# A transformer block's forward and backward pass on one core: token-major q and k by TensorE in place of DMA transposes, and b2 added by VectorE in place of one-row matmuls

## The chip, the core and the metric

The kernel runs on one core of a Trainium2 chip. The metric is the device time of one execution in microseconds (us). The kernel before took 688.7 us (median of three runs, 688.36 to 696.13). One of these executions was recorded by the hardware profiler; its trace is what the readings below rest on.

The engines are called as the profile calls them: PE is TensorE (its weight loads are listed apart as PEld), DVE is VectorE, ACT is ScalarE, POOL is GpSimd, and SP is SyncE, which does nothing here but issue DMAs. SPq, POOLq and ACTq are the streams in which an engine issues DMAs.

## The reference

One pre-norm transformer block over 2048 tokens of 512 features, and the gradients of its output with respect to the input and all weights:

```python
h  = x + attention(layernorm(x)) @ wo          # 32 heads of 16 features
h2 = h + gelu(layernorm(h) @ w1 + b1) @ w2 + b2    # 1792 hidden features
# attention of token s: softmax over the 8 tokens s, s-2, ..., s-14 (those before 0 are masked)
#   logits = q[s] . k[s - 2w] * 16**-0.5 ;  o[s] = sum_w attn[w] * v[s - 2w]
out, vjp = jax.vjp(block, x, wqkv, wo, w1, b1, w2, b2)
return out, *vjp(grad_out)
```

Inputs and outputs are bf16.

## The kernel before

The tokens are worked on in four chunks of 512 (`NC = 4`, `CH = 512`), each of four tiles of 128 (`TPC`). Two layouts are used: feature-major (features on the 128 partitions, tokens along the free dimension, four groups `g` of 128 features) and token-major (tokens on the partitions).

**Phase 1** (0 to about 190 us) is the attention forward pass. `p1_ln` loads x, normalizes it on DVE, and turns it feature-major on PE (`to_fm`: 16 transposes into two PSUM tiles of the pool `psT`, each copied out by ACT). `p1_qk` and `p1_v` project q, k and v feature-major; ACT copies each 128x512 result from PSUM. `dots` multiplies q with eight shifted views of k on DVE (four operations of 128x4096) and sums over the features of a head on PE. `p1_sm1` and `p1_sm2` are the softmax. `p1_o` needs v token-major: v's rows are written to DRAM (`v_d`), and POOL gathers ten shifted rows per partition from there into the tile `R` (`gather_rows`, two gathers per chunk, two tiles). DVE multiplies R with the softmax coefficients (`band`, line 275), PE sums, ACT copies `ost`, POOL stores it, and `unperm` turns it feature-major. `p1_d` multiplies with wo, adds x, and computes the second layer norm; `p1_d2` turns that feature-major for phase 2. `p1_round` sets the program order: `dots(c+1)`, `p1_d(c-1)`, `p1_qk(c+2)`, `p1_o(c)` in two halves with `p1_v(c+1)` between, so that three chunks are in work at a time.

**Phase 2** (about 190 to 395 us) is the feed-forward part, forward and backward. `p2_h` makes the hidden units and gelu; `p2_rest` multiplies with w2, adds b2 and h (line 640 adds b2 as a matmul with one contracted row, line 641 adds h through the identity matrix), stores the output, and runs the backward pass through w2 and w1.

**Phase 3** (from about 395 us) is the attention backward pass. It gathers rows from the token-major q, k and output gradient (`q_d`, `k_d`, `go_d`) as phase 1 does from `v_d`, and fills PE with the weight gradients.

What the change touches:

- *Order of the features.* The band multiplication wants token-major rows in the order (feature within a head, head). The kernel before gets it by reordering the weights: the columns of wqkv are loaded into `wraw` and `wrav` and copied into `wqkv` in the new order by ACT (k and q, four copies) and POOL (v, two copies), and wo's rows are reordered by a DRAM-to-DRAM transfer into `woP_d`, from which phase 3 loads its transpose. As all groups `g` then hold the same heads in the same places, one summing matrix `S32` serves them all.
- *Token-major q and k* (`to_tm_store`, called through `p1_tm` right after `p1_qk`): per chunk and tensor, four DMA transposes from SBUF to SBUF issued by SP, and then SP's stores to DRAM. v does not go this way: `p1_v` transposes it on PE (line 395), ACT copies the result (`vtm`, line 398), SP stores it (line 400). The output gradient goes through `to_tm_pe` in the same manner.
- *The second layer norm's last step* (`layernorm` with `aj`): the multiplication with rstd and the addition of the mean's term, four operations of 128x512 per chunk, run on ACT (line 181); in the first layer norm they run on DVE (line 183).

Each engine executes its instructions in one fixed order. In phases 1 and 2 a scheduler at build time chooses that order from the dependencies and the program order; in phase 3 it is written out by hand. SP issues its DMAs in such an order too, and an instruction that waits holds up all behind it on its engine.

Of the kernel before, what the change touches and what calls it, by code (L numbers as in the profile page):

```python
# [36 lines left out]
def kernel(  # L37
# [70 lines left out]
    make_identity(nc, ident[:])  # L108
    S32 = const.tile([P, 32], BF16, name="S32")
    Sum4 = const.tile([P, P], BF16, name="Sum4")  # L110
    nSum4 = const.tile([P, P], BF16, name="nSum4")
    Sm = const.tile([P, 4, P], BF16, name="Sm")
    mk = const.tile([16, 2, 4, 32], BF16, name="mk")
    ones_row = const.tile([1, P], BF16, name="ones_row")
# [4 lines left out]
    V.memset(ones_row[:], 1.0)  # L119
# [5 lines left out]
    b2row = const.tile([1, D], BF16, name="b2row")  # L125
# [8 lines left out]
    woP_d = dram.tile([D, D], BF16, name="woP_d")  # L134
# [32 lines left out]
    def layernorm(wp, src, rstd_all, c, dst, aj=()):  # L167
        mv = wp.tile([P, TPC, 2], F32, name="mv", tag="mv", bufs=2)
        for j in range(TPC):
            st = wp.tile([P, 6], F32, name="st6", tag="st6", bufs=2)  # L170
            V.bn_stats(out=st[:], in_=src[:, j, :])
            V.bn_aggr(out=mv[:, j, :], in_=st[:])
        rs = rstd_all[:, c * TPC:(c + 1) * TPC]
        ve = wp.tile([P, TPC], F32, name="ve", tag="ve", bufs=2)
        V.tensor_scalar(out=ve[:], in0=mv[:, :, 1], scalar1=EPS, scalar2=None, op0=ALU.add)
        G.tensor_tensor(out=rs, in0=ve[:], in1=mhalf[:], op=ALU.pow)
        nm = wp.tile([P, TPC], F32, name="nm", tag="nm", bufs=2)
        V.scalar_tensor_tensor(out=nm[:], in0=mv[:, :, 0], scalar=-1.0, in1=rs, op0=ALU.mult, op1=ALU.mult)
        for j in range(TPC):
            if j in aj:  # L180
                A.activation(out=dst[:, j, :], in_=src[:, j, :], func=ACT.Identity, scale=rs[:, j:j + 1], bias=nm[:, j:j + 1])
            else:
                V.tensor_scalar(out=dst[:, j, :], in0=src[:, j, :], scalar1=rs[:, j:j + 1], scalar2=nm[:, j:j + 1],
                                op0=ALU.mult, op1=ALU.add)
# [24 lines left out]
    def to_tm_pe(fm, dst, c, stage):  # L209
        for j2 in range(TPC // 2):  # L210
            pt = TT("ptm")
            for jj in range(2):
                for g in range(4):
                    T.transpose(pt[:, jj * 512 + g * P:jj * 512 + (g + 1) * P],
                                fm[:, g, (2 * j2 + jj) * P:(2 * j2 + jj + 1) * P], ident[:])
            st = stage()
            A.copy(out=st[:], in_=pt[:].rearrange("p (a n) -> p a n", a=2))
            r = j2 * 2 * P
            SY.dma_start(out=dst[c][r:r + 2 * P, :].rearrange("(a p) d -> p a d", p=P), in_=st[:])
            if j2 == 0 and c > 0:  # L220
                SY.dma_start(out=dst[c - 1][CH:CH + RPAD, :], in_=st[0:RPAD, 0, :])

    def to_tm_store(wp, fm, off, dst, c, back, nb=2, stage=None):
        st = stage() if stage else wp.tile([P, TPC, D], BF16, name="tmst", tag="tmst", bufs=nb)
        for g in range(4):
            SY.dma_start_transpose(out=st[:, :, g * P:(g + 1) * P], in_=fm[:, g, off:off + CH])
        r = RPAD if back else 0
        SY.dma_start(out=dst[c][r:r + CH, :].rearrange("(a p) d -> p a d", p=P), in_=st[:])
        if back and c + 1 < NC:
            SY.dma_start(out=dst[c + 1][0:RPAD, :], in_=st[P - RPAD:P, TPC - 1, :])  # L230
        if not back and c > 0:
            SY.dma_start(out=dst[c - 1][CH:CH + RPAD, :], in_=st[0:RPAD, 0, :])
# [9 lines left out]
    def dots(wp, ql, kw_, L, mask):  # L242
        for g in range(4):
            pr = wp.tile([P, W, 512], BF16, name="pr", tag="prod", bufs=2 + (wp is not late))
            V.tensor_tensor(out=pr[:], in0=ql[:, g, :].unsqueeze(1).to_broadcast([P, W, 512]),  # L245
                            in1=_sub(kw_[:, g, PAD:PAD + 512], [[-DIL, W], [1, 512]]), op=ALU.mult)
            for hf in range(2):
                for w4 in range(4):
                    T.matmul(L[hf][32 * w4:32 * w4 + 32, :], lhsT=S32[:], rhs=pr[:, 2 * w4 + hf, :],
                             start=(g == 0), stop=(g == 3), skip_group_check=True)  # L250
        if mask:
            for hf in range(2):
                T.matmul(L[hf][:, 0:16], lhsT=mk[:, hf].rearrange("p a b -> p (a b)"), rhs=ident[0:16, 0:16],
                         start=False, stop=True, skip_group_check=True)
# [80 lines left out]
    def p1_ln(c):  # L335
# [3 lines left out]
        if c == 0:  # L339
            wraw = wff.tile([P, 2, DC, D], BF16, name="wraw", tag="w10", bufs=1)  # L340
            wrav = wff.tile([P, DC, D], BF16, name="wrav", tag="w18", bufs=1)
            raws = [wraw[:, 1], wraw[:, 0], wrav[:]]
            for i in (1, 0, 2):
                SY.dma_start(out=raws[i], in_=A_wqkv[:, i * D:(i + 1) * D].rearrange("(a p) j -> p a j", p=P))

            def by_dh(i, put, lo, hi):
                put(out=wqkv[:, :, i * D + lo * H:i * D + hi * H].rearrange("p a (d h) -> p a d h", h=H),
                    in_=raws[i].rearrange("p a (h d) -> p a d h", d=DH)[:, :, lo:hi, :])
            by_dh(1, A.copy, 0, 8)
            by_dh(1, A.copy, 8, 16)  # L350
            by_dh(0, A.copy, 0, 8)
            by_dh(0, A.copy, 8, 16)
            by_dh(2, G.tensor_copy, 0, 8)
            by_dh(2, G.tensor_copy, 8, 16)
        ln1 = early.tile([P, TPC, D], BF16, name="ln1", tag="ln1", bufs=2)
        layernorm(early, xt, rstd1, c, ln1, ())
# [13 lines left out]
    def p1_tm(c):  # L370
        to_tm_store(early, st_[c]["kt"], PAD, k_d, c, True)
        to_tm_store(early, st_[c]["qt"], 0, q_d, c, False)

    def p1_qk(c):
        qt = early.tile([P, 4, CH], BF16, name="qt", tag="qt", bufs=2)
        kt = early.tile([P, 4, PAD + CH], BF16, name="kt", tag="kt", bufs=2)
        if c == 0:
            V.memset(kt[:, :, 0:PAD], 0.0)
            G.dma_start(out=vf_d[:, :, 0:PAD], in_=kt[:, :, 0:PAD])
# [6 lines left out]
        p1_tm(c)  # L386

    def p1_v(c):
        vt = early.tile([P, 4, PAD + CH], BF16, name="vt", tag="vt", bufs=1)
        p1_proj(c, 2, vt, PAD)  # L390
        for j2 in range(TPC // 2):
            pt = TT("ptm")
            for jj in range(2):
                for g in range(4):
                    T.transpose(pt[:, jj * 512 + g * P:jj * 512 + (g + 1) * P],
                                vt[:, g, PAD + (2 * j2 + jj) * P:PAD + (2 * j2 + jj + 1) * P], ident[:])
            st = early.tile([P, 2, D], BF16, name="vtm", tag="vtm", bufs=2)
            A.copy(out=st[:], in_=pt[:].rearrange("p (a n) -> p a n", a=2))
            r = j2 * 2 * P + RPAD
            SY.dma_start(out=v_d[c][r:r + 2 * P, :].rearrange("(a p) d -> p a d", p=P), in_=st[:])  # L400
            if j2 == 1 and c + 1 < NC:
                SY.dma_start(out=v_d[c + 1][0:RPAD, :], in_=st[P - RPAD:P, 1, :])
        G.dma_start(out=vf_d[:, :, PAD + c * CH:PAD + (c + 1) * CH], in_=vt[:, :, PAD:PAD + CH])

# [61 lines left out]
    def p1_d(c):  # L466
# [11 lines left out]
        layernorm(late, ht, rstd2, c, ln2, (0,1,2,3))  # L478
# [6 lines left out]
    p1_ln(0)  # L485
    for j in range(4):
# [4 lines left out]
    for j in range(4):  # L491
        V.tensor_copy(out=Sm[32 * j:32 * j + 32, j, :], in_=Sum4[32 * j:32 * j + 32, :])
    G.memset(mk[:], 0.0)
# [15 lines left out]
    for a_, b_, t_ in w1:  # L509
        G.dma_start(out=t_[:], in_=B_w1[:, a_ * P:b_ * P].rearrange("(a p) f -> p a f", p=P))  # L510
    def p1_round(c):
        if c + 2 < NC:
            p1_ln(c + 2)
        if c == 0:
            for (d_t, r) in ((v_d[0], 0), (k_d[0], 0), (q_d[NC - 1], CH), (go_d[NC - 1], CH)):
                SY.dma_start(out=d_t[r:r + RPAD, :], in_=zrow[:])
            G.dma_start(out=woP_d[:].rearrange("(d h) n -> d h n", h=H), in_=A_wo.rearrange("(h d) n -> d h n", d=DH))
            SY.dma_start(out=b1b[:], in_=B_b1.rearrange("(f p) -> f p", p=P))
            SY.dma_start(out=b2row[:], in_=B_b2.rearrange("(a n) -> a n", a=1))
# [18 lines left out]
        p1_o(c, 1)  # L538
        if c == 1:
# [21 lines left out]
    def load_wT(name, src):  # L561
# [6 lines left out]
               h2s=([P, D], 2), gyr=([P, D], 2), junk=([P, D], 1), u=([P, D], 2),   # L568
# [57 lines left out]
    def p2_rest(c):  # L626
# [8 lines left out]
        load_rows(ln2, ln2_d, c)  # L635
        for j in range(TPC):
# [3 lines left out]
            T.matmul(ps[:], lhsT=ones_row[:], rhs=b2row[:], start=False, stop=False)  # L640
# [45 lines left out]
    def ga_sum(L, pr, g):  # L686
        for hf in range(2):
            for w4 in range(4):
                T.matmul(L[32 * w4:32 * w4 + 32, hf, :], lhsT=S32[:], rhs=pr(2 * w4 + hf),
# [10 lines left out]
    def p3_pre():  # L700
# [7 lines left out]
        to_tm_pe(got, go_d, 0, lambda: ft("tst", "tmst0")[:, 0:8, :].rearrange("p (a b) f -> p a (b f)", a=2))  # L708
        yield
        L = [X("ps_ga0") for _ in range(2)]  # L710
        for g in range(4):
            pr = ft("xa", "pr0")
            ga_prod(pr[:].rearrange("p a b n -> p (a b) n"), got, vw, g)
            for hf in range(2):
                for w4 in range(4):
                    w = 2 * w4 + hf
                    T.matmul(L[hf][32 * w4:32 * w4 + 32, :], lhsT=S32[:], rhs=pr[:, w // 4, w % 4, :],
# [33 lines left out]
    for a_, b_, t_ in w2T:  # L751
        SY.dma_start_transpose(out=t_[:], in_=B_w2[a_ * P:b_ * P, :])
    goT0 = [ft("goT")]
# [29 lines left out]
    for c in range(NC):  # L783
        if c == 2:
            load_wT("woT", woP_d[:])
# [280 lines left out]
    def p3_go(c, at=(1, 2, 3, 4)):  # L1066
# [12 lines left out]
        def t():  # L1079
            to_tm_pe(got, go_d, c, lambda: pt3("tmst"))  # L1080
# [181 lines left out]
```

## Time and profile before

| what | us |
| --- | --- |
| median of three runs | 688.7 |
| the profiled execution | 688.36 |
| its span, first to last instruction | 686.5 |
| PE busy | 605.8 (88%) |
| DVE busy | 511.7 (75%) |
| ACT busy | 372.0 (54%) |
| POOL busy | 148.7 (22%) |
| mean granted PE clock | 0.968 of full |

The 1.9 us between the execution's time and its span lie before the first and after the last instruction. In rows of the trace the columns are: line of the kernel, engine, operation, the tile written and the tiles read (`out<-in`), shape; then busy time and the mean of one in ns, or, in a timeline, start and duration in us. What stands after `<-` in brackets or at a row's end is how long the engine had been idle before that row and what it had waited for. A timeline joins neighbouring instructions of one line into one row (`x2`). A wait for several things is put down to the one that came last.

### The profile page before, as it was taken

The numbers are of one execution on the slowest core, as the hardware profiler recorded it, in microseconds if no ns is written. First come the engines' busy times: TensorE is split into PE (matmuls) and PEld (weight loads), VectorE is DVE, ScalarE is ACT, GpSimd is POOL, SyncE is SP. The second block draws the span as 40 slices with busy tenths as digits, with TensorE's granted clock in tenths as the row PEclk, the third lists the DMA queues.
The fourth block names the chain that finished last, engine by engine and source line by source line (L and its number), as shares of the span: only waits on it lengthen the run. The fifth ranks groups of instructions, "written<-read, shape, count | busy, mean of one in ns | idle before, by whom it ended". The sixth has DMA issues, their size and how long they took to land. (4 is left out here: it accounts for less than half of the span.)

```text
span 686.5 us, 9972 instructions
## 1 busy us (share of the span) xinstructions
PE 605.8 (88%) x3761; PEld 281.1 (41%) x3820; DVE 511.7 (75%) x734; ACT 372.0 (54%) x574; POOL 148.7 (22%) x186
## 2 busy tenths in 40 slices
PE   2888838687699999999999988999999999988997
PEld 1333313233234444444444432434446567533443
DVE  7988838876878886986956878886978798396400
ACT  6576636669976366366333162594377337464311
POOL 6232122243201110110110115130223125030100
PEclk9999969789989999999999999999999999999999
DMA  7989999753699994995995899977599689979141
GB/s 234 232 237 286 232 227 199 270 175 112 150 254 255 249 256 100 236 252 151 238 275 151 230 353 331 362 249 279 181 394 324 240 285 354 322 271 314 70 153 47
DMA packets 165230, 163.58 MB, mean 238 GB/s; under 512 B 111757, under 2 KB 149694, under 8 KB 158526
## 3 DMA queue, kind: packets, MB, share of 16 engines
q1 hardware_dynamic: 137358, 73.78, 43.6%
q0 software_dynamic: 15520, 78.15, 33.6%
q10 hardware_dynamic: 12304, 11.01, 5.0%
q8 instruction: 30, 0.49, 0.3%
q14 instruction: 18, 0.15, 0.1%
HBM read 88.15 MB, written 48.55 MB: 199 GB/s over the span
## 5 line engine op out<-in xcount | busy, mean ns | idle before, releaser
L1045 DVE TENSOR_TENSOR prb<-R,cf 128x2048 bf16<-128x2048 bf16 x96 | 110.9, 1218 | 7.0 <-DMA R<-k_d,rowi 3.0
L189 ACT ACTIVATE gyr<-ps_gl,rstd 128x512 bf16<-128x512 f32 x32 | 21.9, 686 | 84.3 <-PE ps_gl L1108 32.0
L607 PE MATMUL ps_h<-ln2T,w 128*128 128x512 bf16 x219 | 57.1, 394 | 1.3 <-ACT xa L609 0.6
L929 PE MATMUL ps_gw<-gout_r,gwm 128*128 128x512 bf16 x216 | 52.8, 387 | 3.3 <-DMA gwm<-gT_d 2.8
L639 PE MATMUL ps_f<-w,gt 128*128 128x512 bf16 x220 | 53.0, 387 | 2.7 <-ACT ln2T L165 2.0
L652 PE MATMUL ps_gg<-goT,w2T 128*128 128x512 bf16 x219 | 53.9, 379 | 0.6 <-issue 0.2
L937 PE MATMUL ps_gw<-gwm,ln_r 128*128 128x256 bf16 x448 | 53.0, 273 | 1.0 <-ACT gwst L856 1.0
L663 PE MATMUL ps_gl<-w1T,dt 128*128 128x512 bf16 x218 | 50.9, 379 | 0.8 <-ACT gyr L189 0.4
L366 PE MATMUL ps_qkv<-ln1T,wqkv 128*128 128x512 bf16 x185 | 48.3, 399 | 3.7 <-ACT ln1T L165 2.6
L275 DVE TENSOR_TENSOR prb<-R,cf 128x2048 bf16<-128x2048 bf16 x32 | 37.6, 1212 | 18.7 <-DMA R<-v_d,rowi 18.7
L683 DVE TENSOR_TENSOR pr<-got,vw 128x4096 bf16<-128x4096 bf16 x16 | 36.3, 2289 | 16.2 <-ACT got L680 11.4
L654 DVE CUSTOM_DVE_ANT_0 dt<-ps_gg,dt 128x512 bf16<-128x512 f32 x56 | 37.7, 685 | 13.4 <-PE ps_gg L652 8.4
L937 PEld LDWEIGHTS <-ln_r 128*128 128x128 bf16 x448 | 42.6, 98 | 12.4 <-issue 6.5
L608 ACT ACTIVATE xb<-ps_h,b1c 128x512 bf16<-128x512 f32 x56 | 39.0, 698 | 11.6 <-PE ps_h L607 8.8
L957 PE MATMUL ps_gwq<-gqh,ln_r 128*128 128x512 bf16 x188 | 42.2, 379 | 0.8 <-ACT gwst L856 0.6
L609 ACT ACTIVATE xa<-ps_h,b1c 128x512 bf16<-128x512 f32 x56 | 38.9, 701 | 5.0 <-DVE dt L620 5.0
L592 POOL DMA_DIRECT2D gT_d<-tst x16 | 12.1, 755 | 123.7 <-DMA tst<-gt 123.3
L1055 ACT ACTIVATE gks<-ps_band 128x512 bf16<-128x512 f32 x32 | 19.0, 597 | 36.0 <-PE ps_band L1053 31.5
L245 DVE TENSOR_TENSOR pr<-qt,kt 128x4096 bf16<-128x4096 bf16 x16 | 35.9, 2283 | 0.7 <-PE ps_band L280 0.4
L293 ACT COPY gqkvT<-ptu 128x1024 bf16<-128x1024 bf16 x24 | 24.3, 1011 | 18.6 <-PE ptu L292 18.6
L607 PEld LDWEIGHTS <-w 128*128 128x128 bf16 x224 | 22.2, 101 | 29.4 <-issue 6.8
L614 ACT ACTIVATE xa<-xa 128x2048 bf16<-128x2048 bf16 (+1 forms) x16 | 27.2, 1697 | 13.0 <-DVE xa L613 12.9
(181 smaller groups left out, 1117.8 us busy)
## 6 DMA issues: line engine op xcount, KB each, us to landing
gwm<-ghT_d SPq DMA_DIRECT2D x7, 1024.0 KB
gT_d<-tst POOLq DMA_DIRECT2D x12, 512.0 KB, 4.7
ghT_d<-tst POOLq DMA_DIRECT2D x12, 512.0 KB, 4.8
gwm<-gT_d SPq DMA_DIRECT2D x6, 1024.0 KB
out_dram<-gwst ACTq DMA_DIRECT2D x22, 256.0 KB
ln_d<-ln POOLq DMA_DIRECT2D x8, 512.0 KB, 7.6
vw<-vf_d SPq DMA_DIRECT2D x4, 528.0 KB
xt<-in_A_x_dram SPq DMA_DIRECT2D x4, 512.0 KB
```

The source lines that it names most:

```text
L366: T.matmul(ps[:], lhsT=wqkv[:, dc, sel * D + g * P:sel * D + (g + 1) * P], rhs=st_[c]["ln1T"][:, dc, :], start=(dc == 0), stop=(dc == DC - 1))
L607: T.matmul(ps[:], lhsT=wcol(w1, dc, f), rhs=ln2T[c][:, dc, :], start=(dc == 0), stop=(dc == DC - 1))
L608: A.activation(out=xb[:, f - f0, :], in_=ps[:], func=ACT.Identity, bias=b1c[:, f:f + 1])
L609: A.activation(out=x2[:, f - f0, :], in_=ps[:], func=ACT.Square, bias=b1c[:, f:f + 1])
L639: T.matmul(ps[:], lhsT=gts[f // 4][:, f % 4, j * P:(j + 1) * P], rhs=wrow(w2, f), start=(f == 0), stop=False)
L652: T.matmul(ps[:], lhsT=wcol(w2T, dc, f), rhs=goT[:, dc, :], start=(dc == 0), stop=(dc == DC - 1))
L654: V.tensor_tensor_reduce(out=dsl, in0=ps[:], in1=dsl, scale=1.0, scalar=0.0, op0=ALU.mult, op1=ALU.add, accum_out=gb1p[:, f, c:c + 1])
L663: T.matmul(ps[:], lhsT=dts[f // 4][:, f % 4, j * P:(j + 1) * P], rhs=wrow(w1T, f), start=(f == 0), stop=(f == FT - 1))
L929: yield from mm_pair("ps_gw2", lambda ps, o, u, i, t, k: T.matmul(ps[:], lhsT=g_[:, o, i * HN + t, :], rhs=gout_r[i][:, t, :], **k), MM, w ...
L937: yield from mm_pair("ps_gw1", lambda ps, o, u, i, t, k: T.matmul(ps[:, 256 * u:256 * u + 256].rearrange("p (a f) -> p a f", a=2), lhsT=ln ...
L957: yield from mm_pair("ps_gwq", lambda ps, o, u, i, t, k: T.matmul(ps[:], lhsT=ln1_r[i][:, t, (2 * d2 + o) * P:(2 * d2 + o + 1) * P], rhs=h ...
L1045: V.tensor_tensor(out=pr[:, 4 * hf:4 * hf + 4].rearrange("p j (d h) -> p j d h", h=H), in0=R[:, o:o + 4, :].rearrange("p j (d h) -> p j d ...
```

## The change

The features keep their natural order (head, feature). wqkv is loaded straight into place and wo is used as it is. The reordering moves into the transposes that make rows token-major: their second operand is a permutation matrix `Pmat` in place of the identity, and they write PSUM in runs of eight elements. One function, `to_tm_store`, now does this for q, k, v and the output gradient, on PE with copies on ACT and stores issued by SP. In the sums over a head's features, `S32` becomes one matrix per group (`Emat`). `p1_tm` moves from the end of `p1_qk` to the end of `p1_round`. The second layer norm's last step goes to DVE. b2 is loaded once, repeated over all partitions, and added to h by one DVE operation per chunk.

```diff
+    Pmat = const.tile([P, P], BF16, name="Pmat")
+    ind8 = const.tile([P, 8], BF16, name="ind8")
+    Emat = const.tile([P, 4, 32], BF16, name="Emat")
...
-            if j in aj:
-                A.activation(out=dst[:, j, :], in_=src[:, j, :], func=ACT.Identity, scale=rs[:, j:j + 1], bias=nm[:, j:j + 1])
-            else:
-                V.tensor_scalar(out=dst[:, j, :], in0=src[:, j, :], scalar1=rs[:, j:j + 1], scalar2=nm[:, j:j + 1],
-                                op0=ALU.mult, op1=ALU.add)
+            V.tensor_scalar(out=dst[:, j, :], in0=src[:, j, :], scalar1=rs[:, j:j + 1], scalar2=nm[:, j:j + 1],
+                            op0=ALU.mult, op1=ALU.add)
...
-    def to_tm_store(wp, fm, off, dst, c, back, nb=2, stage=None):
-        st = stage() if stage else wp.tile([P, TPC, D], BF16, name="tmst", tag="tmst", bufs=nb)
-        for g in range(4):
-            SY.dma_start_transpose(out=st[:, :, g * P:(g + 1) * P], in_=fm[:, g, off:off + CH])
-        r = RPAD if back else 0
-        SY.dma_start(out=dst[c][r:r + CH, :].rearrange("(a p) d -> p a d", p=P), in_=st[:])
...
+    def to_tm_store(wp, fm, off, dst, c, back, nb=3, stage=None):
+        for j2 in range(TPC // 2):
+            pt = TT("ptm")
+            for jj in range(2):
+                j = 2 * j2 + jj
+                for g in range(4):
+                    T.transpose(_sub(pt[:], [[32, DH], [1, 8]], jj * 512 + 8 * g),
+                                fm[:, g, off + j * P:off + (j + 1) * P], Pmat[:])
+            st = stage() if stage else wp.tile([P, 2, 512], BF16, name="tmst", tag="tmst", bufs=nb)
+            A.copy(out=st[:], in_=pt[:].rearrange("p (a n) -> p a n", a=2))
+            r = j2 * 2 * P + (RPAD if back else 0)
+            SY.dma_start(out=dst[c][r:r + 2 * P, :].rearrange("(a p) d -> p a d", p=P), in_=st[:])
...
-                    T.matmul(L[hf][32 * w4:32 * w4 + 32, :], lhsT=S32[:], rhs=pr[:, 2 * w4 + hf, :],
+                    T.matmul(L[hf][32 * w4:32 * w4 + 32, :], lhsT=Emat[:, g, :], rhs=pr[:, 2 * w4 + hf, :],
...
-            by_dh(1, A.copy, 0, 8)
...
-            by_dh(2, G.tensor_copy, 8, 16)
+            for i in range(3):
+                o = (1, 0, 2)[i] * D
+                SY.dma_start(out=wqkv[:, :, o:o + D], in_=A_wqkv[:, o:o + D].rearrange("(a p) j -> p a j", p=P))
...
-        layernorm(late, ht, rstd2, c, ln2, (0,1,2,3))
+        layernorm(late, ht, rstd2, c, ln2)
...
+    V.tensor_copy(out=_sub(Pmat[:], [[1, 8], [8, DH]]), in_=_sub(ident[:], [[DH, 8], [1, DH]]))
...
         p1_o(c, 1)
+        p1_tm(c + 1)
...
+        V.tensor_tensor(out=h_all[c][:], in0=h_all[c][:], in1=b2b[:].unsqueeze(1).to_broadcast([P, TPC, D]), op=ALU.add)
         for j in range(TPC):
...
-            T.matmul(ps[:], lhsT=ones_row[:], rhs=b2row[:], start=False, stop=False)
             T.matmul(ps[:], lhsT=ident[:], rhs=h_all[c][:, j, :], start=False, stop=True)
...
+    b2b = ft("b2b")
+    A.dma_start(out=b2b[:], in_=_ap(B_b2, [[0, P], [1, D]]))
...
-            load_wT("woT", woP_d[:])
+            load_wT("woT", A_wo)
```

## The prediction, made before the changed kernel was run

> **What bounds the kernel now.** I read the table by stages first. Cut at the kernel's own seams, its rows give us, then busy us (and instructions) of PE, PE weight loads, DVE, ACT and POOL, granted clock, DMA share, GB/s:
>
> ```profile
> 20.00:46.00 26.00, 21.68 (x162) 9.81 (x162) 23.61 (x40) 16.48 (x28) 5.57 (x7) 1.00 1.08 248
> 46.00:84.00 38.00, 33.56 (x246) 13.73 (x249) 33.98 (x41) 25.31 (x41) 11.77 (x15) 0.96 0.93 251
> 84.00:122.00 38.00, 23.41 (x175) 9.95 (x174) 21.95 (x19) 18.88 (x30) 9.81 (x14) 0.82 0.94 211
> 122.00:150.00 28.00, 19.19 (x142) 8.46 (x136) 21.68 (x33) 18.38 (x28) 10.88 (x15) 0.82 0.68 233
> 150.00:190.00 40.00, 28.92 (x158) 12.48 (x161) 31.01 (x44) 36.62 (x51) 12.09 (x16) 0.89 0.56 139
> 190.00:212.00 22.00, 21.73 (x86) 8.68 (x87) 16.49 (x20) 14.36 (x23) 0.00 (x0) 0.89 1.16 227
> 212.00:395.00 183.00, 180.17 (x841) 77.83 (x857) 147.48 (x283) 87.30 (x149) 23.05 (x31) 1.00 0.90 219
> ```
>
> From 190 us on PE is 98% busy: a matmul saved there is time saved. Before 190 nothing is full for long. DVE leads to 84 us; from 84 to 122 every engine idles, DVE for 16 of 38 us; ACT is nearly full from 150 to 190. So phase 1 must be read by its waits (total us, times, longest):
>
> ```profile
> POOL R L237 <- DMA v_d<-vtm: 22.6, 2, 12.1
> DVE prb L275 <- DMA R<-v_d,rowi: 18.7, 6, 5.7
> DVE nm L178 <- POOL rstd L176: 8.9, 4, 5.8
> ```
>
> Then the timeline of the hole at 84 us:
>
> ```profile
> 67.18 1.93 ACT L398 COPY vtm<-ptm 128x1024 bf16<-128x1024 bf16 x2 [0.70 <-PE ptm L395]
> 76.86 1.26 SPq L226 DMA_TRANSPOSE tmst<-qt  x1
> 78.29 0.47 SPq L228 DMA_DIRECT2D k_d<-tmst  x1
> 80.56 1.80 SPq L400 DMA_DIRECT2D v_d<-vtm  x2
> 85.96 1.05 POOL L237 DMA_INDIRECT R<-v_d,rowi  x1 [12.08 <-DMA v_d<-vtm]
> 88.32 1.05 POOL L176 TENSOR_TENSOR rstd<-ve,mhalf 128x4 f32<-128x4 f32 x1
> 96.29 4.63 DVE L275 TENSOR_TENSOR prb<-R,cf 128x2048 bf16<-128x2048 bf16 x4 [5.73 <-DMA R<-v_d,rowi]
> ```
>
> v's rows were ready at 69.1, but SP sent them only at 80.56, after the k and q transposes and stores ahead of them in its order. POOL stood 12.08 us on them, with the next layer norm's rstd behind the gather, and DVE stood for both.
>
> **The change, part by part.** The sum is made against the profiled execution's own 688.36 us (span 686.5); the median of the three runs, 688.7, lies 0.3 above. A difference under 2% (13.8 us) is about what a measurement of this kernel cannot tell from none.
>
> *T1, the weights arrive in place.* Four ACT copies (7.84 us, 5.95 to 13.79) and two POOL copies (11.12 to 15.14) go. PE's transposes of the first chunk end at 12.1, ln1T's copies start only at 13.70 behind the weight copies, and PE waits 2.65 us on them. DVE's setup copies beside POOL's are slow (nSum 1.90, each Sm 0.73, against 0.20 for Sum); whether that was POOL's doing is open. Added on DVE: six small setup operations and two memsets, about 0.2 us each by the Sum row. Value -2; bounds -4 (all 5 us of slow setup shrinking, less the additions) and 0 (the additions eat it). The reordered copy of wo in DRAM goes too, at nothing: it was a 10 us transfer that nobody waited for.
>
> *T2, v's rows no longer queue behind transposes.* SP loses 32 transposes and has only stores and loads in phase 1. In the new order v of the next chunk follows q's stores of the chunk before, whose tiles are ready long before, so v would leave at about 69; by the present 3.5 us from last issue (82.4) to gather (85.96) POOL could start at 74, where it is free (73.9), and R lands 9.4 us later (median), at 83.4. DVE is ready at 83.64. The DVE waits in question are 2.15 (first chunk, at 55.33), 5.76 for nm, 5.73 and 3.56 for R (second), 2.96 (third): 20.2 in all. Bounds -20.2, and -4 if R's landing, up to 17.0 us, is the wall. I take -15, nearest to the second chunk's 15.05, because in the other two DVE runs into ACT soon after.
>
> The Trainium skill, "Advanced Engine Details and Errata", section "X-Bar Transpose (TRN2)", speaks against this term: transposing DMAs are there as fast as plain ones, at 350 to 400 GB/s. An estimate from that: 128 KB take 0.37 us, a chunk's eight take 3 us, so v would be held for 3 us, T2 would be about -4 and the sum 681. The trace differs: SP alone spends 1.2 to 1.4 us in most of them and up to 6.4.
>
> *T3, k and q become token-major on PE and ACT.* Per chunk 32 more transposes and four more 128x1024 evacuations. The same work is in the trace for go and v: 4.9 us for 64 transposes (0.077 each) and 1.013 per copy.
>
> ```profile
> L398 ACT COPY vtm<-ptm 128x1024 bf16<-128x1024 bf16 x8 | 7.7, 1013 | 0.7 <-PE ptm L395 0.7
> L181 ACT ACTIVATE ln<-h,nm,rstd 128x512 bf16<-128x512 bf16 x16 | 11.7, 807 | 8.9 <-DVE nm L178 5.8 <-issue 3.1
> L183 DVE TENSOR_SCALAR ln<-xt,rstd,nm 128x512 bf16<-128x512 bf16 x16 | 5.6, 401 | 0.1
> ```
>
> That is 2.5 us of PE and 4.06 of ACT a chunk, 16.2 of ACT in all. Cover: ACT idles 51 of the 130 us from 20 to 150. But p1_tm sits in front of p1_d, and ACT's order becomes oT, three tmst copies, one h, a tmst, two ln1T, then the other h tiles; DVE's statistics wait for h. The transposes share psT's two buffers with pt and ptu, and the fourth copy of a burst needs the first one's staging tile back (three tiles) from a store like vf_d<-vt, which lands in 5.1 us. Bounds: 0, and 2.5 + 4.06 + 5.1 = 11.7 a chunk, 47 in all, if the whole turn is serial. I take +6, 1.5 a chunk, nearer the covered end because the dots (9.2 us of DVE) run beside it. The transposes through Pmat write PSUM in runs of eight; no row shows that. The nearest is a strided PSUM read, natural() at 597 ns against 584 for a plain one, so I put nothing on it (bounds 0, and 0.077 again on 256 of them, 20 us).
>
> *T4, the second layer norm's apply moves from ACT to DVE.* Four 0.35 on DVE in place of four 0.73 on ACT (2.93 per chunk). Chunks 0 and 1 fall where DVE leads: +1.4 each. Chunk 2's copies (157.20 to 160.13) stand in a full ACT: -2.9. Chunk 3's (183.87 to 186.80) are in the chain that lets PE start phase 2 at 189.55: -1.5. Sum -1.6; bounds -6 (both full ACT stretches gain their 2.93) and +5.6 (all on DVE).
>
> "Perfetto Trace Analysis", section "Optimizing Scalar/DVE Operations", says of such work that it may pay to move it off a saturated DVE. By that rule T4 would be +5.6 and the sum 677; the stage rows show ACT fuller than DVE where the last two chunks' norms run.
>
> *T5, b2.*
>
> ```profile
> 206.44 3.19 PE L639 MATMUL ps_f<-w,gt 128*128 128x512 bf16 x14
> 209.56 0.38 PE L640 MATMUL ps_f<-b2row,ones_row 1*128 1x512 bf16 x1
> 209.88 0.39 PE L641 MATMUL ps_f<-h,ident 128*128 128x512 bf16 x1
> 210.10 2.11 PE L607 MATMUL ps_h<-ln2T,w 128*128 128x512 bf16 x9
> ```
>
> The fourteen matmuls start 0.216 apart, so the last starts at 209.25; L641 starts 0.63 later, and 0.22 of that would remain. Each one-row matmul costs 0.41, not 0.38: 16 x 0.41 = 6.6, all on a full PE (bounds 3.5, at 0.22 each, and 6.6). Added: four DVE additions of 128x2048, 1.22 each by L1045's row, all four early in phase 2, and a 128 KB load that ACT issues. They wait behind nothing but the load; behind them on DVE stands the next gelu block, whose xb ACT and then PE wait for. Cover: DVE idles 5.5 of 22 us there. Value +0.5, bounds 0 and 4.9.
>
> Phase 3 issues the same work (only go's transposes change their matrix).
>
> Sum: -2 - 15 + 6 - 1.6 - 6.6 + 0.5 = -18.7; 688.36 - 18.7 = 669.7, against the median **670**.
>
> **Rivals.**
> *ACT takes the stall's place* (T3 at ACT's full 16.2): -8.5, 680. For: ACT evacuates everything in phase 1. Against: its 51 idle us.
> *The change doesn't do what it frees* (T2 -4): the gather's landing stays late, -7.7, 681. For: DMA share is 0.94, and a second gather always follows the first. Against: the share falls to 0.68 at 122 to 150, where the transposes have ended.
> *Slower: the token-major turn is serial.* Place: between the second half of p1_o and p1_d, every chunk; PE in order waits for psT, ACT for the staging tile, DVE for h. Price 11.7 a chunk, 47: with the other terms as forecast (-24.7) that gives +22, 711. It decides from (13.8 + 24.7)/4 = 9.6 us a chunk. For: psT has two buffers and five users. Against: v's identical turn (68 to 70 us) cost PE no visible wait.
>
> **How the numbers follow.** Forecast 0.50, ACT 0.19, landing 0.16, serial turn 0.15. The forecast's own width, half the T2 span, is some 656 to 682, so a fifth of it lies above 675, and a fifth of the two middle rivals below: faster 0.47, same 0.38, slower 0.15. The range goes from 656 (T1, T2 and T4 near their lower ends) over the rivals to 703.
>
> **What would show it.** Right: no DVE wait for R over 3 us near the second chunk; v's store within 2 us of its copies; clock from 84 to 122 near 1.0; phase 2 starting near 177; phase 2 shorter by 6 us. Wrong: ACT waiting for staging tiles, PE waiting on ACT tmst, DVE on h; transposes slower than 0.08 us; PE waiting for xb after 190.

## The result, and the profile after

The changed kernel takes 665.0 us (median of four runs, 663.6 to 666.6) beside 691.0 for the kernel before: a ratio of 0.9616, 95% interval 0.9548 to 0.9684, so 22 to 31 us less. The forecast was 670. The profiled execution has a span of 662.1 us where the one before had 686.5, 24.4 less; the sum had said 18.7. A ratio, here and below, leaves out runs more than 1.5% above the fastest of their kernel, which a median keeps in. The profiled execution of the kernel before took 688.4 us, the least of its four (to 696.1), so differences of spans come out smaller than ratios say.

The table by stages of the changed kernel, cut at its own seams (columns as before: us, busy us of PE, PE weight loads, DVE, ACT and POOL, granted clock, DMA share, GB/s):

```profile
44.00:75.00 31.00, 28.87 (x254) 13.38 (x257) 28.81 (x26) 24.05 (x36) 10.80 (x12) 1.00 0.60 200
75.00:106.00 31.00, 27.56 (x230) 12.77 (x237) 27.05 (x35) 23.96 (x38) 13.60 (x15) 1.00 0.64 215
106.00:131.00 25.00, 19.19 (x169) 9.91 (x164) 22.83 (x36) 18.14 (x28) 11.21 (x15) 0.97 0.85 299
131.00:170.00 39.00, 31.87 (x173) 13.23 (x176) 32.51 (x51) 32.47 (x48) 10.91 (x14) 0.88 0.54 136
170.00:193.00 23.00, 18.92 (x78) 7.99 (x79) 20.82 (x25) 15.50 (x23) 0.00 (x0) 0.93 1.20 224
193.00:373.00 180.00, 176.57 (x833) 77.95 (x848) 149.18 (x286) 86.61 (x147) 23.89 (x31) 1.00 0.97 229
```

A round of phase 1 now takes 31 us where it took 38, and DVE is busy for 28.8 and 27.1 of them: the hole at 84 us, where DVE worked 22 of 38 us, is filled. The DMA share of these rounds fell from 0.93 to 0.60 while the bytes per second fell only from 251 to 200; that will matter below. The first ps_f matmul comes at 170.4 us (before 189.5), and the end of phase 2 (last ps_gl) at 372.8 (before 395.6).

The waits of the first 200 us, where the kernel before had 22.6, 18.7 and 8.9 us in these three:

```profile
DVE nm L177 <- POOL rstd L175: 5.9, 7, 1.2
...
DVE prb L263 <- DMA R<-v_d,rowi: 1.5, 1, 1.5
POOL R L225 <- DMA v_d<-tmst: 1.3, 1, 1.3
```

The timeline of the second chunk's v and its gather:

```profile
63.34 1.93 ACT L214 COPY tmst<-ptm 128x1024 bf16<-128x1024 bf16 x2 [0.75 <-ACT vt L344]
...
64.38 1.27 SPq L216 DMA_DIRECT2D v_d<-tmst  x2
...
69.75 2.57 POOL L225 DMA_INDIRECT R<-v_d,rowi  x1 [0.60 <-DVE pr L233]
...
80.03 1.19 DVE L263 TENSOR_TENSOR prb<-R,cf 128x2048 bf16<-128x2048 bf16 x1
```

v leaves as soon as its first copy is done, the gather starts at 69.75 (before 85.96), and DVE begins the products at 80.03 (before 96.29) without a wait for R. The costs of the turn and of the layer norm, in the table of groups:

```profile
L214 ACT COPY tmst<-ptm 128x1024 bf16<-128x1024 bf16 x32 | 31.3, 1020 | 6.1 <-PE ptm L211 3.2 <-ACT vt L344 1.6 <-ACT ost L426 1.0
L211 PE MATMUL ptm<-Pmat,kt 128*128 128x128 bf16 x64 | 5.1, 219 | 0.4 <-ACT tmst L214 0.4
L179 DVE TENSOR_SCALAR ln<-h,rstd,nm 128x512 bf16<-128x512 bf16 x16 | 5.5, 406 | 0.0
```

The transposes through Pmat take 0.080 us each for k; those of the output gradient take 4.9 us for 64 in both kernels, through the identity before and through Pmat now: writing PSUM in runs of eight costs nothing that shows here. PE waited 0.4 us for ACT's copies of k.

And b2's place in the stream of PE:

```profile
184.63 3.19 PE L612 MATMUL ps_f<-w,gt 128*128 128x512 bf16 x14
187.65 0.38 PE L613 MATMUL ps_f<-h,ident 128*128 128x512 bf16 x1
187.86 3.19 PE L612 MATMUL ps_f<-w,gt 128*128 128x512 bf16 x14
```

From the last of the fourteen to the matmul of h it is one ordinary step of 0.22 us (before 0.63).

### The profile page after: what moved, and what is told of

Same layout as the page of the kernel before. It is cut to its first block, busy times and chain, and to the rows that moved or that the text cites. A ratio compares the mean times of both kernels' runs of the same rounds, so it can differ in the third digit from the quotient of the medians.

```text
span 662.1 us, 10168 instructions
## 1 busy us (share of the span) xinstructions
PE 600.9 (91%) x3870; PEld 286.2 (43%) x3932; DVE 518.4 (78%) x761; ACT 366.8 (55%) x570; POOL 152.3 (23%) x183
## 5 line engine op out<-in xcount | busy, mean ns | idle before, releaser
L1019 DVE TENSOR_TENSOR prb<-R,cf 128x2048 bf16<-128x2048 bf16 x96 | 110.8, 1219 | 10.2 <-DMA R<-k_d,rowi 5.6
L612 PE MATMUL ps_f<-w,gt 128*128 128x512 bf16 x219 | 51.1, 379 | 1.8 <-DVE gt L587 1.6
L903 PE MATMUL ps_gw<-gout_r,gwm 128*128 128x512 bf16 x215 | 51.4, 380 | 0.8 <-issue 0.6
L1027 PE MATMUL ps_band<-prb,S 128*32 128x512 bf16 x384 | 30.5, 385 | 5.1 <-DVE prb L1019 4.7
L214 ACT COPY tmst<-ptm 128x1024 bf16<-128x1024 bf16 x32 | 31.3, 1020 | 6.1 <-PE ptm L211 3.2
L586 ACT ACTIVATE xa<-xa 128x2048 bf16<-128x2048 bf16 (+1 forms) x16 | 27.1, 1700 | 13.3 <-DVE xa L585 13.2
```

The costliest lines, as they stand in the source:

```text
L612: T.matmul(ps[:], lhsT=gts[f // 4][:, f % 4, j * P:(j + 1) * P], rhs=wrow(w2, f), start=(f == 0), stop=False)
L903: yield from mm_pair("ps_gw2", lambda ps, o, u, i, t, k: T.matmul(ps[:], lhsT=g_[:, o, i * HN + t, :], rhs=gout_r[i][:, t, :], **k), MM, w ...
L1019: V.tensor_tensor(out=pr[:, 4 * hf:4 * hf + 4].rearrange("p j (d h) -> p j d h", h=H), in0=R[:, o:o + 4, :].rearrange("p j (d h) -> p j d ...
```

## The experiments

Each ratio is to the kernel before, measured on the same chip; 1% is 6.9 us.

### The turn, as a whole: away, and on TensorE

The first question was how much of the gain is k's and q's turn. One kernel leaves it out:

```diff
-        for g in range(4):
-            SY.dma_start_transpose(out=st[:, :, g * P:(g + 1) * P], in_=fm[:, g, off:off + CH])
+        st = fm[:, :, off:off + CH]
```

> The kernel before, with q's and k's turn left out: SP stores the feature-major tiles themselves (512 KB each, the same packets of 1 KB) at the same place in the program, so the rows that phase 3 gathers are not the right ones. This is T2 without T3. By the forecast -15 (673 to 675), and T3, the price of the turn on TensorE and ACT, is this time against the kernel with that turn (672.4): by the forecast 6 us, so this kernel would lie at 666. If it lies at 672, the turn on TensorE and ACT costs nothing.

The other turns q and k as v is turned, all three through one function, with the identity:

```diff
...
+                    T.transpose(pt[:, jj * 512 + g * P:jj * 512 + (g + 1) * P],
+                                fm[:, g, off + j * P:off + (j + 1) * P], ident[:])
...
-        p1_tm(c)
...
+        p1_tm(c + 1)
```

> The kernel before, with q's and k's token-major rows made by TensorE transposes (plain identity, (d, h) order kept) and ACT copies at the end of the round, as v's are: terms T2 and T3 of the prediction together, without T1, T4, T5 and without the permuting matrix. By the forecast -15 + 6 = -9, so 679; by what the changed kernel's trace shows (phase 2 starts 19 us earlier, and no wait on the staging tiles) rather -14 to -18, so 670 to 674. If the time lies at 679 or above, T1 or T4 carried more of the gain than I put there. The rival 'ACT takes the stall's place' expects ACT waits on tmst or DVE waits for h that the changed kernel avoids only by its DVE layer norm: 680 or more.

Without any turn: 669.9 us, ratio 0.9673 (0.9594 to 0.9753), span 671.9, 14.6 less than in the profiled execution before (the profiled execution of this kernel took 673.7 us, its other three 667.7 to 670.1). With the turn on TensorE: 672.4 us, ratio 0.9718 (0.9667 to 0.9769), span 670.6. So the DMA transposes cost 17 to 28 us by the ratio, the new turn costs some 3 by the ratios and -1.3 by the spans, which is not distinguishable from nothing, and these two terms alone are about 19.5 of the 26.5 us.

### Was it SP's order?

The prediction's account was that v's stores stood behind transposes in SP's order. The first test moves them to ACT's queue:

```diff
-            SY.dma_start(out=v_d[c][r:r + 2 * P, :].rearrange("(a p) d -> p a d", p=P), in_=st[:])
+            A.dma_start(out=v_d[c][r:r + 2 * P, :].rearrange("(a p) d -> p a d", p=P), in_=st[:])
```

> The kernel before, with one thing changed: v's rows are stored by DMAs that ACT issues instead of SP; q and k still go through the DMA transposes, in their old place. Theory 'order': what cost the time was v's stores standing behind eight transposes in SP's order. Then v_d leaves within 2 us of its copies in every chunk (before 80.56 us in the second chunk, 11.5 us after the copies), DVE's waits for R (18.7 us in all) fall under 6, and the span falls by 10 to 15 us, to 672 to 677. Rival 'load': the transposes slow the DMA engines for everybody, so v's store lands as late and the gather takes as long as before; R's waits stay above 12 us and the span falls by less than 5 us, to 682 or more.

687.0 us, ratio 0.9899 (0.9856 to 0.9941): 4 to 10 us, between the two theories. In its trace ACT stood 15.2 us on a transpose of k. I took that for the buffer of k that ACT was to write again, and gave k and q a third one (the transposes then write into tiles that phase 2 needs later):

```diff
...
-        qt = early.tile([P, 4, CH], BF16, name="qt", tag="qt", bufs=2)
-        kt = early.tile([P, 4, PAD + CH], BF16, name="kt", tag="kt", bufs=2)
+        qt = ln2T[1] if c == 0 else early.tile([P, 4, CH], BF16, name="qt", tag="qt", bufs=2)
+        kt = early.tile([P, 4, PAD + CH], BF16, name="kt", tag="kt", bufs=3)
...
```

> The earlier kernel with v's rows stored through ACT's queue left one wait in place of v's: ACT stood 15.2 us on the transposes of k, whose tile (one of two buffers) it was to write again. Here k and q have a third buffer too (q of the first chunk lies in a tile that phase 2 needs later, and the transposes write into two such tiles). So v does not wait for SP and ACT does not wait for the transposes, but all 32 transposes run. Theory 'SP is the narrow place': they cost only by holding what waits for SP, so the gain is nearly that of taking them away, -13 to -18 (671 to 676). Rival 'load': they slow loads, stores and gathers beside them, so the gain stays at that of the earlier kernel, -5 to -9 (680 to 684).

690.8 us, ratio 0.997 (0.992 to 1.002): nothing gained, and the same wait. The timeline of ACT in this kernel shows what I had misread:

```profile
68.12 1.93 ACT L398 COPY vtm<-ptm 128x1024 bf16<-128x1024 bf16 x2 [0.70 <-PE ptm L395]
83.87 1.67 ACTq L400 DMA_DIRECT2D v_d<-vtm  x2
87.02 0.30 ACTq L402 DMA_DIRECT2D v_d<-vtm  x1
87.36 0.59 ACT L446 CAST rb<-ps_r 128x512 bf16<-128x512 f32 x1 [17.30 <-DMA ln2T<-kt]
```

The wait is put at the copy of rb, but it belongs to the store before it: v_d left at 83.87, 14 us after its last copy had ended. The semaphores in this trace show why. A DMA counts up a completion semaphore when it lands; in this kernel the DMAs of SP and of ACT take eight of them in turn (numbers 101 to 104, 106, 115, 117 and 118), and an issue waits until the DMA that had its semaphore before has landed. v's three stores were to use 104, 106 and 115. These had last been given to transposes that SP issued at 81.26, 82.58 and 83.88 and that landed at 83.79, 85.10 and 87.00; the stores left at 83.87, 85.17 and 87.02. So on ACT's queue v was still behind the transposes, and now ACT with it. Neither run tests what it was meant to, and what gained 4 to 10 us in the first of them stays open.

Moving the call of p1_tm in the source, with the DMA transposes kept, tests nothing either:

```diff
-        p1_tm(c)
...
+        p1_tm(c + 1)
```

> The kernel before, with the DMA transposes of q and k kept but issued at the end of the round, behind v's stores, where the changed kernel has its turn through TensorE. Theory 'order': as for v on another queue, 10 to 15 us less (672 to 677), since v is sent first and nobody waits for q's and k's rows in this stage. Rival 'load': the same 32 transposes still run beside the gathers of the next chunk, so the gain is under 5 us (682 or more). A third way: SP comes late to the next chunk's loads or to v of the chunk after, because it is still busy with transposes; then a new wait shows at v_d or at xt, and the span is 680 to 690.

691.7 us, ratio 0.9999 (0.9972 to 1.0026). The scheduler put SP's DMAs of phase 1 in exactly the order they had before, v's stores of the second chunk leaving at 81.70. It serves as a measure of the noise: two kernels with the same order of DMAs differ by less than 0.3%.

POOL's DMAs have semaphores of their own (107 to 114 in this kernel's trace), so a store issued there waits for no transpose:

```diff
-            SY.dma_start(out=v_d[c][r:r + 2 * P, :].rearrange("(a p) d -> p a d", p=P), in_=st[:])
+            G.dma_start(out=v_d[c][r:r + 2 * P, :].rearrange("(a p) d -> p a d", p=P), in_=st[:])
```

> The kernel before, with v's rows stored by DMAs that POOL issues. On ACT's queue v's store was not freed: in the second chunk it left at 83.9 us, 15 us after its copies, because its completion semaphore had last been used by one of SP's transposes and the issue waited for that one. POOL's DMAs use semaphores of their own, so here v waits for no transpose in any way, while all 32 still run. Theory 'order': v_d of the second chunk leaves by 72 us, the gather at 75 to 77, R's waits fall to 3 to 7 us, and the span falls by 10 to 15 us (672 to 677). Rival 'load': with transposes in flight v's store and the gather land late all the same: the first product of the second chunk stays at 92 us or later (before 96.3; without transposes 82.2), and the span falls by less than 5 us.

686.7 us, ratio 0.9880 (0.9821 to 0.9939): 4 to 12 us of the 17 to 28. The ten runs lie between 676.9 and 694.7, and the trace is of one that took 678.1. In it v of the second chunk left at 68.00 and 72.47, the gather started at 78.85, and the first product came at 89.92: 6.4 us earlier than before, 7.7 later than without transposes (82.24). What remains shows in the stage tables, the first of this kernel:

```profile
46.00:65.00 19.00, 17.29 (x128) 7.00 (x128) 12.63 (x12) 13.47 (x22) 9.34 (x9) 1.00 1.10 198
65.00:84.00 19.00, 14.78 (x107) 6.57 (x108) 18.18 (x23) 8.91 (x13) 8.51 (x10) 0.73 1.04 265
105.00:121.00 16.00, 13.40 (x103) 5.46 (x98) 15.11 (x19) 10.73 (x18) 9.56 (x12) 1.00 1.05 216
```

and the second of the kernel with no turn:

```profile
46.00:65.00 19.00, 18.17 (x143) 7.40 (x139) 18.50 (x19) 14.12 (x24) 7.25 (x8) 1.00 0.71 255
65.00:84.00 19.00, 16.64 (x119) 7.08 (x119) 18.07 (x27) 13.77 (x22) 11.72 (x9) 1.00 0.66 224
105.00:121.00 16.00, 12.63 (x101) 5.94 (x100) 15.29 (x22) 14.11 (x22) 6.80 (x5) 0.79 0.59 229
```

The second figure from the right is the DMA share. With transposes the sixteen engines are full (1.04 to 1.10) and over the three stretches together move no more bytes than they do at 0.59 to 0.71 without. A gather caught in that can take long:

```profile
46.81 2.99 POOL L237 DMA_INDIRECT R<-v_d,rowi  x1 [0.31 <-issue]
...
64.62 4.63 DVE L275 TENSOR_TENSOR prb<-R,cf 128x2048 bf16<-128x2048 bf16 x4 [5.75 <-DMA R<-v_d,rowi]
```

17.8 us from issue to the product that waited for it, and 17.8 again at 115.51 to 133.33; without transposes the two gathers that DVE waited for took 12.1 and 7.5. But the other three that DVE waited for beside the transposes took 9.6 to 11.1, and the median landing is alike with and without them (9.4 us in the kernel before, 9.9 with no turn; the longest 17.0 and 11.3): the load lengthens some gathers, not all. So the order is worth about 8 of some 22 us by the ratios (10.2 of 14.6 by the spans, of executions at opposite ends of the two kernels' runs), and the load has a part in the rest. That the rest is all the load isn't shown: POOL's second store also came 4.5 us after the first, behind a store of the layer norm's rows that waited 3.0 us for DVE, and its gather later than the changed kernel's.

### The weights

```diff
-                SY.dma_start(out=raws[i], in_=A_wqkv[:, i * D:(i + 1) * D].rearrange("(a p) j -> p a j", p=P))
...
+                SY.dma_start(out=wqkv[:, :, o:o + D], in_=A_wqkv[:, o:o + D].rearrange("(a p) j -> p a j", p=P))
```

> The kernel before, with wqkv loaded straight into place and no reordering copies on ACT and POOL: T1 alone. It leaves out the new order of the weights' columns, so what it computes is a different attention of the same size. By the forecast -4 to 0: the first kt copy at 15.6 us in place of 17.5 and DVE's setup copies at 0.2 to 0.35 us each in place of 0.7 to 1.9. As the first chunk is 2 us earlier, but v of the second chunk still waits behind the transposes, the rival is that the 2 us are gone at the hole at 84 us: the span within 1 us of 686.5.

690.5 us, ratio 0.9988 (0.9940 to 1.0037). The first kt copy came at 15.25 (before 17.5), but v still left behind the transposes: POOL stood 27.9 us on its rows, 15.7 at the longest. By the second chunk the two us are gone, as the rival had it: its first product came at 103.07, beside 96.29 before.

### The second layer norm

On the kernel before, T4 alone:

```diff
-        layernorm(late, ht, rstd2, c, ln2, (0,1,2,3))
+        layernorm(late, ht, rstd2, c, ln2)
```

> The kernel before, with the second layer norm's last step on DVE: T4 alone. By the forecast -1.6 (687; phase 2 would start 1.5 us earlier, at 188). The rival 'DVE is the fuller engine' gives +5.6 (694). A third: ACT had stood in the way of the hole at 84 us too, and the gain is -4 to -6 (683 to 685).

685.5 us, ratio 0.9881 (0.9784 to 0.9978): 1.5 to 15 us less, nearer to the third expectation than to the forecast, which the interval does not exclude. So it was undone in the changed kernel, with the opposite diff:

> The changed kernel, with the second layer norm's last step back on ACT: T4 undone. By the forecast +1.6 (666.5 beside 665.0). By the traces: the kernel before with the turn on TensorE needs 246.0 us from the first hidden-unit matmul to the end of phase 2, the changed one 238.1, and b2 alone gave 6.3 of it, which leaves 1.6. Rival 'DVE is the fuller engine' (DVE is 28.8 us busy of 31 from 44 to 75): -2 to -5.6, 659 to 663. Third: +4 to +6, ACT's copies in phase 1 then being late everywhere.

671.4 us, ratio 0.9702 (0.9648 to 0.9756) beside 0.9616: 6 us slower, the third expectation again. The intervals of the two ratios overlap; the times do not (668.0 to 674.5 beside 663.6 to 666.6). Its timeline shows where the operations stand:

```profile
140.67 2.93 ACT L180 ACTIVATE ln<-h,nm,rstd 128x512 bf16<-128x512 bf16 x4
...
170.36 2.93 ACT L180 ACTIVATE ln<-h,nm,rstd 128x512 bf16<-128x512 bf16 x4 [0.36 <-DVE nm L177]
...
174.99 1.91 ACT L164 COPY ln2T<-pt 128x1024 bf16<-128x1024 bf16 x2
```

The third chunk's four operations follow other work on ACT without a gap, and the last chunk's stand between the layer norm and the last ln2T, which the changed kernel copies at 169.05. The first ps_f moves from 170.4 to 176.0.

If the first two chunks cost DVE time, a mixture should beat both:

```diff
-        layernorm(late, ht, rstd2, c, ln2)
+        layernorm(late, ht, rstd2, c, ln2, (0, 1, 2, 3) if c < 2 else ())
```

> The changed kernel, with the second layer norm's last step on ACT for the first two chunks, where DVE is the fuller engine, and on DVE for the last two, where ACT is. By T4's own working the first two chunks cost 1.4 each on DVE, so -2.8: 662. If the order of T4's working is wrong (ACT's lateness is paid in every chunk), +1 to +3.

670.9 us, ratio 0.9689 (0.9640 to 0.9738): no better than all on ACT. Its last ln2T starts at 174.62 although no layer norm runs on ACT there. The scheduler orders ACT's and DVE's work anew as soon as these operations move, so whether the first two chunks' operations or the new order cost the 5 us stays open. What falls is my division by chunks, and with it the reading that the last two chunks' operations on ACT explain the 6 us: here they are on DVE, and the first ps_f still comes at 175.7.

### b2

On the kernel before:

```diff
+        V.tensor_tensor(out=h_all[c][:], in0=h_all[c][:], in1=b2b[:].unsqueeze(1).to_broadcast([P, TPC, D]), op=ALU.add)
...
-            T.matmul(ps[:], lhsT=ones_row[:], rhs=b2row[:], start=False, stop=False)
```

> The kernel before, with b2 added by one DVE operation per chunk and the sixteen one-row matmuls gone: T5 alone. By the forecast -6.6 + 0.5 = -6.1, so 682 to 683 beside 688.5 to 691. The changed kernel's trace shows its phase 2 only 3.7 us shorter, so the rival is that DVE's additions give 2 to 3 us back (each holds the next gelu block): -3 to -4. If nothing is saved (0 to -1), the one-row matmuls ran where PE waited anyway.

685.7 us, ratio 0.9893 (0.9827 to 0.9959). From the first hidden-unit matmul to the end of phase 2 its trace has 240.8 us (391.6 - 150.8) where the kernel before has 247.1 (395.6 - 148.5): 6.3 less, the forecast's 6.1. Undone in the changed kernel:

> The changed kernel, with b2 added by sixteen one-row matmuls again and without DVE's four additions: T5 undone. By the forecast +6.1 (671); the kernel before with b2 on DVE was shorter by 6.3 to 6.8 us between the first hidden-unit matmul and the end of phase 2. Rival: the parts don't add up (the turn on TensorE alone reached 0.972 of the time before, and undoing the layer norm's move alone cost 6 us of the changed kernel's gain), so part of b2's gain is spent on waiting in the changed kernel: +1 to +3.

665.4 us, ratio 0.9655 (0.9619 to 0.9691) beside 0.9616: some 3 us by the ratios, 0.4 by the medians, which is not distinguishable from nothing and far from the forecast's 6.1. The row of the first stretch of phase 2 in this kernel:

```profile
170.00:193.00 23.00, 22.74 (x97) 9.27 (x96) 16.35 (x23) 16.48 (x24) 0.00 (x0) 0.96 1.11 241
```

Here PE is busy for 22.7 of 23 us and DVE for 16.4; with b2 on DVE it is 18.9 and 20.8. From the first hidden-unit matmul to the end of phase 2 the changed kernel still needs 5.5 us less than this one (238.1 beside 243.6), but 3.8 of these lie before the first ps_f, where no b2 is added; from the first ps_f on it is 202.4 beside 204.1, 1.7 less. And the two profiled executions differ the other way before the first hidden-unit matmul (2.0 us) and in phase 3 (2.6, where DVE waits 5.6 us for R<-k_d beside 2.3). Whether the earlier start of phase 3 only meets loads that come no earlier, or the executions just differ by so much, was not tested.

## Why the prediction was right, and where its steps were not

The forecast was 669.7, against 664.3 for the profiled execution. The side and the range were right, and the turn carried most of the gain. But its two terms were forecast at -9 and measured at -19.5 together, and the total lies as near as it does partly by luck, since T1 and T5 brought some 5 us less than their terms. Two figures of the prediction do not follow from its working: half of T2's span (20.2 to 4) is 8 us, which gives 662 to 678 and not 656 to 682, and the serial rival's own 711 lies above the range's end of 703.

- **T1**, -2, bounds -4 to 0. Measured alone -0.8 (-4.1 to +2.6). The 2 us are there in the trace and are not seen in the time.
- **T2**, -15, "v's rows no longer queue behind transposes". The size holds by the spans (-14.6) and is too small by the ratio (-22.6, beyond its bound of -20.2). The step that failed is the reason: I read the hole as a matter of SP's order, and ordering accounts for about 8 (4 to 12). The transposes also filled the DMA engines, and beside them two of the eight gathers took 17.8 us; how much of the rest that explains stays open. The rival "the gather's landing stays late" named that effect, but took it as independent of the change; its own evidence, a DMA share of 0.94 that falls to 0.68 where the transposes end, was the right row, and I used it only against the rival. The Trainium skill's statement that transposing DMAs are as fast as plain ones ("Advanced Engine Details and Errata", section "X-Bar Transpose (TRN2)") does not agree with the load here either: without them the packets of SP's queue take 40.3% of 671.9 us in place of 43.6% of 686.5, so 28.5 us of all sixteen engines for 4.2 MB, 147 GB/s. By the same measure POOL's queue, which transposes nothing, moves 78.15 MB in 33.4% of 671.9 us, 348 GB/s.
- **T3**, +6, bounds 0 to 47. Measured about +3 by ratios and -1.3 by spans: near its lower bound. ACT made 16 us more of these copies in its idle time, as the cover had it; staging tiles were not waited for, and PSUM buffers for 1.2 us in all (PE on tmst). "ACT takes the stall's place" and the serial turn are both excluded by the kernel with the turn on TensorE alone, at 672.4.
- **T4**, -1.6, bounds -6 to +5.6. Measured -5.9 to -6.4 in the changed kernel, at the lower bound. The sign was right and the size wrong: I charged the first two chunks +2.8 that the mixture didn't find. The mechanism (a full ACT near the start of phase 2) is not confirmed either, since the mixture keeps these operations off ACT there and is as slow; what makes the 6 us stays open. The Trainium skill's suggestion that it may pay to move work off a saturated DVE ("Perfetto Trace Analysis", section "Optimizing Scalar/DVE Operations") would have left the first two chunks' operations on ACT, where DVE is busy for 27.1 of 31 and 22.8 of 25 us; doing so made this kernel some 5 us slower.
- **T5**, -6.1. Right on the kernel before (6.3 in its phase); in the changed kernel 0.4 to 3. What did not hold there is "Cover: DVE idles 5.5 of 22 us there": in the first stretch of phase 2 DVE is busy for 20.8 of 23 us with the additions, and PE for only 18.9, where it is busy for 22.7 without them. That the four additions made PE's holes isn't shown: the longest, 3.2 us up to 180.78, is a wait for ACT, which had itself waited 4.0 us, to 177.74, for DVE's gelu, and the first addition starts at 179.63.

By ratios the parts are: turn -19.5, layer norm -5.9, b2 -2.7, together -28.1, where the whole is -26.5; the intervals cover the difference. Of the signs named beforehand, the R waits, v's store and the clock from 84 to 122 (1.00) were as said; phase 2 began not at 177 but at 170.4, and it became shorter by 3.7 us and not by 6 (from the first ps_f to the last ps_gl 202.4 beside 206.1).

## What to carry to other kernels

Here a transposing DMA cost three things: its issuer's time (1.2 to 6.4 us of SP each in the kernel before), a place before whatever shared its queue or completion semaphores, and the DMA engines, where a high busy share at an unchanged byte rate gave it away. TensorE, and ACT that copies from PSUM, had idle time, and there the same turn cost some 3 us, which is not distinguishable from nothing. Before a wait is put down to order, look at what the transfer does to the others in flight, and test order with a store that shares no queue and no semaphore. And a gain measured alone on a full engine is not the gain in a kernel whose other changes have moved the bound: undo each part in the final kernel.

## What the runs showed that was not expected

- 32 DMA transposes of 128 KB made 17 thousand packets of some 240 bytes (the kernel before against the one with no turn); SP was held up to 9.96 us in one (in the kernel with v on ACT's queue and three buffers).
- A wait is shown at the next compute instruction of an engine: a DMA issue ahead of it, waiting for a completion semaphore, was the one that waited (17.3 us on ACT).
- DVE's setup copies beside POOL's weight copies took 1.90 us (nSum) and 0.73 (each Sm); in the changed kernel, without those, 0.20 and 0.33.
